# Step sizes behind the first keys, 95 small products ahead of the first Gram, and two value scalings moved to ScalarE

## The chip, the cores and the metric

The kernel runs on one core of a Trainium2 chip. The metric is the device time of one launch in microseconds. Three runs of the kernel before took 745.34, 745.85 and 746.86, median 745.85.

## The reference

Three layers follow each other, all in float32. The first is a delta-rule recurrence over 768 tokens for 4 batches of 8 heads with head size 48; the changed part lies in it:

```python
k_n = k / (np.linalg.norm(k, axis=-1, keepdims=True) + 1e-06)
state = np.zeros((B, H, D, D))
for t in range(S):
    kt, vt, bt = k_n[:, :, t], v[:, :, t], beta[:, :, t, None]
    y[:, :, t] = np.einsum('bhd,bhde->bhe', q[:, :, t], state)
    v_old = np.einsum('bhde,bhd->bhe', state, kt)
    state = state + bt[:, :, :, None] * np.einsum('bhd,bhe->bhde', kt, vt - v_old)
```

A gated layer (384 to 1024, tanh-gelu, a norm, a 768x768 mix over the tokens, 512 to 384, residual) and a second layer with token shift, squared relu and a sigmoid gate follow.

## The kernel before

The recurrence is worked in 12 steps of 64 tokens, two steps to a group. The keys are not normalised; the values are multiplied by the norms of their keys instead. For each group of two steps PE multiplies the keys with each other (`gram`, L320 to L346: two row halves and two block rows per head pair, written as 64x32 products), ScalarE copies the result out of PSUM (L342), and DVE inverts the 32x32 triangles in one long series of small operations (`solver`, L358 to L447). The solver makes the norms first (`neT`, L372), then reads the step sizes `beta_sb` (L380), and ends with a transposed inverse (L440) that PE needs for the group's steps. A product with float32 operands is executed as two products in the trace.

The order of the work on PE, ScalarE, DVE and GpSimd is the order in which the program emits it; each engine takes its own list from the front and waits where an operand is missing. The sync engine's DMA issues are a list of the same kind. At the start the program emits, in this order: the two beta loads (L283), the keys of steps 0 and 1 (L267), memsets of DVE and GpSimd (L299 to L318), two weight blocks (L160), the q of step 0 (L279), values and keys by token of step 0 (L273, L274), and the first Gram in eight jobs. Of these, four jobs for the diagonal blocks come first and feed the solver; the four others feed the coupling of the blocks.

Beside that, weight blocks are split into a rounded part and a rest by "jobs" (`narrow`, L154): a load, a step of ScalarE (L164), four of DVE (L169 to L175), an add on GpSimd (L177), a rounding on ScalarE (L120) and a subtraction on GpSimd (L123). Two jobs are in work at a time, and their steps are strewn between the solver's.

While the first solver is emitted, a list `rest` is emitted beside it, one entry per turn of the loop at L806: the other four jobs of the first Gram, the first products of step 0, and the second group's Gram. The values of steps 0 and 1 are multiplied by their norms in `scale_v` (L464), one GpSimd operation of 128x768 each: step 0 inside the solver (L437), step 1 as the first task after it (L816). The zeros for warm-up products of PE (`keep_warm`, L721) are written by DVE inside the first solver as well (L435).

Of the kernel before, what the change touches and what calls it, by code (L numbers as in the profile page):

```python
# [7 lines left out]
F32 = mybir.dt.float32  # L8
# [3 lines left out]
AF = mybir.ActivationFunctionType  # L12
# [8 lines left out]
P = 128  # L21
C = 64
NG = 6
NU = 32
NPR = 16
# [6 lines left out]
SLOT0 = 3.3  # L32
LOW0 = 1
WARM = 4
SV = 60
B0 = 1.0
PRE = 0.8
GRAM0 = 7
# [35 lines left out]
def vw(t, off, dims):  # L74

    a = t[:]
    return bass.AP(a.tensor, a.offset + off, [list(a.ap[0])] + [list(d) for d in dims])
# [9 lines left out]
def fused_kernel(  # L87
# [17 lines left out]
    nc = tc.nc  # L105
    V, A, G, T = nc.vector, nc.scalar, nc.gpsimd, nc.tensor
# [124 lines left out]
    def slot(tag, shape, dtype=F32):  # L231
        return wq.tile(shape, dtype, name="s" + tag, tag=tag)
# [16 lines left out]
    with ExitStack() as at:  # L249
        ap1 = at.enter_context(tc.tile_pool(name="ap1", bufs=1, side="right"))  # L250
# [8 lines left out]
        kT, kt, vt = {}, {}, {}  # L259
# [3 lines left out]
        def load_k(s):  # L263
            if s >= 12:
                return
            kT[s] = kTb[s % NKT]
            nc.sync.dma_start(out=kT[s], in_=kt_d[s])  # L267

        def load_tok(s):
            t = ap2.tile([P, 2, NPR, D], F32, name="vk")  # L270
            vt[s], kt[s] = t[:, 0], t[:, 1]
            for h in range(2):
                nc.sync.dma_start(out=t[64 * h:64 * h + 64, 0], in_=vk[64 - 64 * h:128 - 64 * h, s, 0])  # L273
            nc.sync.dma_start(out=t[:, 1], in_=vk[:, s, 1])  # L274
# [3 lines left out]
                r = 64 * (1 - h)  # L278
                nc.sync.dma_start(out=SQ[o][s % 2][h][r:r + D, :, D:], in_=q_d[s, o, h])  # L279

        beta_sb = ap1.tile([P, NG, 32], F32, name="beta_sb")
        for h in range(2):
            nc.sync.dma_start(out=beta_sb[64 * h:64 * h + 64], in_=beta[64 - 64 * h:128 - 64 * h])  # L283

        banks = [ps2]

        def bank():
            return banks[0].tile([P, 8, C], F32, name="ms", bufs=3 if banks[0] is ps2 else None)

        Sps = [ps1.tile([P, 8, D], F32, name=f"sps{o}") for o in range(2)]  # L290
        warm = ap1.tile([P, P], mybir.dt.bfloat16, name="warm")
        load_k(0)
        load_k(1)
        NT, GD, Dm = (slot(x, [P, 32, 32]) for x in G0[:3])
        tmp = slot(G0[3], [P, 1024])
        GLb = [slot(G0[4], [P, NU, 32]), slot(W0[2], [P, NU, 32]),
# [52 lines left out]
        GDs, GLs, DTs, neTs, joined = {}, {}, {}, {}, set()  # L349
# [8 lines left out]
        def solver(g):  # L358

            V.transpose(out=NT, in_=GDs[g])  # L360
            G.memset(Yt, 0.0)
            yield 1.14
            ss = ap1.tile([P, 32], F32, name="ss")
            V.tensor_scalar(ss, vw(NT, 0, [(33, 32)]), -1.0, 1e-36, op0=ALU.mult, op1=ALU.max)
            yield 0.2
            ne = yield from rsqrt(ap1, ss, 32, "rn")
            V.tensor_tensor(ne, ne, ss, op=ALU.mult)
            yield 0.2
            V.tensor_scalar(ne, ne, EPS, None, op0=ALU.add)
            yield 0.2  # L370
            neT = ap2.tile([P, 32], F32, name="neT")
            V.transpose(out=neT, in_=ne)  # L372
            neTs[g] = neT
            rn = ap1.tile([P, 32], F32, name="rn")
            V.reciprocal(rn, ne)
            yield 0.4
            V.tensor_tensor(rn, rn, rn, op=ALU.mult)
            yield 0.2
            c = ap1.tile([P, 32], F32, name="c")
            V.tensor_tensor(c, rn, beta_sb[:, g], op=ALU.mult)  # L380
            yield 0.2

            V.tensor_copy(vw(Yt, 0, [(64, 4), (9, 8)]), c.rearrange("p (m i) -> p m i", m=4))
            yield 0.1
            for m in range(4):
                blk = NT[:, 8 * m:8 * m + 8, 8 * m:8 * m + 8]
                V.tensor_tensor(blk, blk, vw(c, 8 * m, [(1, 8), (0, 8)]), op=ALU.mult)
                yield 0.15  # L390

            def total(o_ap, tv, t):
                V.tensor_reduce(out=o_ap, in_=tv, axis=AX.X, op=ALU.add)  # L393
                return t

            for i in range(1, 8):
                tv, t = product(32 * i, [(264, 4), (0, i), (1, i)], NT,
                                0, [(64, 4), (8, i), (1, i)], Yt)
                yield t
                yield total(vw(Yt, i, [(64, 4), (8, i)]), tv, t)  # L400
            V.tensor_copy(vw(Dm, 0, [(264, 4), (32, 8), (1, 8)]), vw(Yt, 0, [(64, 4), (1, 8), (8, 8)]))
            yield 0.4
            V.tensor_copy(vw(NT, 16, [(264, 2), (32, 8), (1, 8)]), vw(Yt, 0, [(64, 2), (8, 8), (1, 8)]))
            yield 0.3
            for dst in (0, 1):
                for p in range(2):
                    o = 16 * p
                    if dst == 0:
                        tv, t = product(32 * (o + 8) + o, [(32, 8), (0, 8), (1, 8)], NT,
                                        128 * p, [(0, 8), (8, 8), (1, 8)], Yt)  # L410
                        ov = vw(NT, 8 + 528 * p, [(1, 8), (32, 8)])
                    else:
                        tv, t = product(33 * (o + 8), [(32, 8), (0, 8), (1, 8)], Dm,
                                        8 + 528 * p, [(0, 8), (32, 8), (1, 8)], NT)
                        ov = vw(Dm, 32 * (o + 8) + o, [(32, 8), (1, 8)])
                    yield t
                    yield total(ov, tv, t)
                    if dst and p == 0:
                        V.tensor_copy(vw(NT, 24, [(1, 8), (32, 8)]), ov)
                        yield 0.2  # L420
            for last in (0, 1):
                if last == 0:
                    ops = [(vw(Yt, 16 * j, [(1, 16), (16, 4)]),
                            (32 * 16 + j, [(32, 16), (0, 4), (1, 16 - j)], NT,
                             16 + 33 * j, [(0, 16), (32, 4), (1, 16 - j)], NT))
                           for j in (12, 8, 4, 0)]
                else:
                    ops = [(vw(Dm, 32 * (16 + i), [(32, 4), (1, 16)]),
                            (32 * (16 + i) + 16, [(32, 4), (0, 16), (1, i + 4)], Dm,
                             0, [(0, 4), (16, 16), (1, i + 4)], Yt)) for i in (0, 4, 8, 12)]  # L430
                for i, (ov, args) in enumerate(ops):
                    tv, t = product(*args)
                    yield t
                    if g == 0 and last and i == 1:
                        V.memset(warm, 0.0)  # L435
                    if g == 0 and last and i == 2:
                        scale_v(0)  # L437
                    yield total(ov, tv, t)
            DT = DTb[g % 2]
            V.transpose(out=DT.rearrange("p u i -> p i u"), in_=Dm)  # L440
            DTs[g] = DT
            yield 1.14
            if g:
                p = point[0] + LAGC
                p += -p % 6 if p % 6 > 2 else 0
                for k in range(2):
                    later.append((p + 6 * k, lambda k=k: couple(g, k)))  # L447
# [16 lines left out]
        def scale_v(s):  # L464
            G.tensor_tensor(vt[s], vt[s], vw(neTs[s // 2], NPR * (s % 2), [(1, NPR), (0, D)]),
                            op=ALU.mult)

        RQs, ysts = {}, {}

# [127 lines left out]
        def after(n, f):  # L597
            later.append((point[0] + n, f))
# [187 lines left out]
        for o in range(2):  # L786
            load_q(0, o)
        load_tok(0)
        diag = gram(0, ((0, 32), (32, 64)))
        for job in diag[:4]:  # L790
            for _, f in job:
                f()
            early(1, NPRE)
        streams.append([point[0], solver(0), "solve"])
        for s in range(2, NKT):
            load_k(s)

        def whole(job):
            for _, f in job:
                f()  # L800
# [3 lines left out]
        rest = [lambda j=j: whole(j) for j in diag[4:]]  # L804
        k = 0
        while any(e[2] == "solve" for e in streams):  # L806
            early(1, PRE)
            k += 1
            if k == 2:
                load_tok(1)  # L810
                for o in range(2):
                    load_q(1, o)
                nc.sync.dma_start(out=g_sb, in_=g_ln)
                nc.sync.dma_start(out=mu_sb, in_=mu)
            if 0 in neTs and 1 not in GDs:
                after(SV, lambda: scale_v(1))  # L816
                body = st_rq(0, 0)
                rest.append(lambda: next(body))
                rest += [lambda j=j: whole(j) for j in gram(1)]
            if rest:  # L820
                rest.pop(0)()
        for f in rest:
# [420 lines left out]
```

## Time and profile before

| | |
|---|---|
| runs (us) | 745.34, 745.85, 746.86 |
| span of the profiled execution (us) | 745.5; no other time of it is given |
| PE busy | 690.3 us, 93%, 10832 products |
| DVE, ScalarE, GpSimd busy | 514.1, 367.9, 201.6 us |
| granted clock over the span | 0.982 |

PE is the busiest engine, but busy time is a mean over stages with different limits. The first of the 40 slices of the span show PE at 2 to 9 tenths and DVE at 6 to 9, the last twenty PE at 9. The span counts from the first to the last instruction of the profiled execution.

### The profile page before, as it was taken

The page shows a single profiled execution, that of the slowest core. Times are in us where ns is not written, and L with a number is a line of the kernel's source. Part 1 is how long each engine was busy: PE and PEld are TensorE (multiplying, and loading weights), DVE is VectorE, ACT ScalarE, POOL GpSimd, SP SyncE. Part 2 cuts the span into 40 slices and gives each one's busy share as a digit, 9 for nine tenths or more (in the row PEclk, how much of TensorE's full clock was granted, in tenths as well). Part 3 has the DMA queues.
Part 4 walks back from the last instruction along what each step waited for, and adds up shares of the span by engine and source line. Part 5 has one row for each costly group of instructions (what it writes and reads, how often), then busy time and mean ns, then how long its engine had stood idle before and what let it go on. Part 6 is the DMA issues. An engine that isn't in the chain of part 4 may idle for free.

```text
span 745.5 us, 24942 instructions
## 1 busy us (share of the span) xinstructions
PE 690.3 (93%) x10832; PEld 641.5 (86%) x10832; DVE 514.1 (69%) x1070; ACT 367.9 (49%) x752; POOL 201.6 (27%) x253
## 2 busy tenths in 40 slices
PE   2668789999998999899999999999999999999998
PEld 2537568878886987779999999999999999999997
DVE  6989999898998695642476857599556565563341
ACT  2226656766675676774331413149445354452240
POOL 3033534454444265463131515330000000000000
PEclk9988989999999899999999999999999999999999
DMA  8503443575565565848763645268000000000000
GB/s 237 133 30 85 130 109 102 165 211 144 144 193 146 151 185 160 231 139 234 236 229 103 189 134 168 84 204 222 33 11 21 33 11 23 22 11 32 16 17 33
DMA packets 81550, 88.76 MB, mean 119 GB/s; under 512 B 24704, under 2 KB 64320, under 8 KB 81440
## 3 DMA queue, kind: packets, MB, share of 16 engines
q1 hardware_dynamic: 76384, 77.72, 35.2%
q0 software_dynamic: 5056, 9.44, 4.7%
q8 instruction: 85, 1.39, 0.8%
q14 instruction: 25, 0.20, 0.1%
HBM read 56.60 MB, written 25.82 MB: 111 GB/s over the span
## 4 chain that ended last, share of the span: by engine, by line
PE 74%; DVE 17%; issue 3%; ACT 2%; DMA 1%; POOL 1%; SPq 1%; POOLq 0%; DVEq 0%; ACTq 0%
PE ms L151 39%; PE ms L960 13%; PE ms L687 5%; DVE sg L355 5%; PE ms L635 4%; DVE sg L393 3%; PE ms L563 2%; DVE Yt L393 2%; PE rk L521 1%; PE ms L456 1%; PE rk L534 1%; PE sps L549 1%; PE rk L498 1%; PE ms L333 1%; PE ms L726 1%
## 5 line engine op out<-in xcount | busy, mean ns | idle before, releaser
L151 PE MATMUL ms<-wvh,sl 128*128 128x384 f32 x192 | 64.6, 336 | 0.0
L151 PE MATMUL ms<-wvl,sh 128*128 128x384 f32 x192 | 64.5, 336 | 0.0
L151 PE MATMUL ms<-wvh,sh 128*128 128x384 f32 x192 | 64.5, 336 | 0.0
L151 PE MATMUL ms<-xm_hi,sw0h 128*128 128x384 f32 x192 | 64.2, 335 | 0.0
L151 PE MATMUL ms<-xm_hi,sw0l 128*128 128x384 f32 x192 | 64.2, 334 | 0.0
L151 PE MATMUL ms<-xm_lo,sw0h 128*128 128x384 f32 x192 | 64.2, 334 | 0.0
L1059 ACT ACTIVATE gh<-w 128x384 fp32r<-128x384 f32 x32 | 16.8, 526 | 93.4 <-DVE w L1058 93.4
L177 POOL TENSOR_TENSOR na<-na,raw 128x256 int32<-128x256 int32 (+2 forms) x43 | 36.5, 849 | 96.0 <-ACT gh L1059 40.7
L123 DVE TENSOR_TENSOR sl<-sg,sh 128x384 fp32r<-128x384 f32 x64 | 35.7, 558 | 30.2 <-ACT sh L120 30.2
L120 ACT ACTIVATE sh<-sg 128x384 fp32r<-128x384 f32 x64 | 33.5, 524 | 36.4 <-DVE sg L1163 36.4
L960 PE MATMUL ms<-sw0h,g 128*128 128x384 f32 x192 | 50.2, 335 | 0.0
L960 PE MATMUL ms<-ws1h,g 128*128 128x384 f32 x192 | 49.9, 334 | 0.0
L355 DVE TENSOR_TENSOR sg<-sg,Yt 128x512 f32<-128x512 f32 (+10 forms) x78 | 46.8, 599 | 1.8
L1179 DVE TENSOR_TENSOR sg<-sg,ms 128x384 f32<-128x384 f32 x24 | 13.3, 555 | 44.9 <-PE ms L151 44.9
L1163 DVE TENSOR_TENSOR sg<-sg 128x384 f32<-128x384 f32 x64 | 35.4, 553 | 10.9 <-ACT sg L1162 10.9
L1162 ACT ACTIVATE sg<-ms 128x384 f32<-128x384 f32 x64 | 30.7, 480 | 22.9 <-PE ms L151 22.9
L514 POOL TENSOR_SCALAR_AFFINE_SELECT SQ<-SQ 64x512 f32<-64x512 f32 x36 | 27.0, 749 | 50.9 <-ACT SQ L513 49.8
L120 ACT ACTIVATE xm_hi<-sg 128x384 fp32r<-128x384 f32 x48 | 23.1, 517 | 34.6 <-PE ms L151 30.5
L687 PE MATMUL ms<-xl,wiu_hi 128*128 128x256 f32 x144 | 39.7, 297 | 0.0
L687 PE MATMUL ms<-xh,wiu_lo 128*128 128x256 f32 x144 | 38.7, 292 | 0.1
L333 PEld LDWEIGHTS ms<-kT 64*32 64x32 f32 x640 | 20.0, 131 | 21.7 <-issue 13.9
L335 PE MATMUL ms<-kT 64*32 64x64 f32 (+1 forms) x640 | 23.3, 235 | 16.5 <-issue 16.5
(246 smaller groups left out, 2241.1 us busy)
## 6 DMA issues: line engine op xcount, KB each, us to landing
u_d<-ug SPq DMA_DIRECT2D x24, 256.0 KB, 4.6
u<-u_d SPq DMA_DIRECT2D x16, 384.0 KB, 4.3
vn_d<-v SPq DMA_DIRECT2D x22, 256.0 KB, 2.8
vk<-in_vk_dram SPq DMA_DIRECT2D x24, 192.0 KB, 3.6
vk<-in_vk_dram SPq DMA_DIRECT2D x12, 384.0 KB, 4.5
out_dram<-sg SPq DMA_DIRECT2D x24, 192.0 KB, 1.9
kT<-in_kt_d_dram SPq DMA_DIRECT2D x8, 512.0 KB
SQ<-in_q_d_dram SPq DMA_DIRECT2D x36, 96.0 KB, 4.0
```

Source lines behind the costliest of these rows:

```text
L120: A.activation(hi, src, AF.Copy)
L123: eng_lo.tensor_tensor(lo, src, hi.bitcast(F32), op=ALU.subtract)
L151: T.matmul(pt, lhsT=a, rhs=b, start=(i == 0), stop=(i == n - 1))
L177: G.tensor_tensor(a.bitcast(I32), a.bitcast(I32), w_lo.bitcast(I32), op=ALU.add)
L333: T.matmul(gps[r:r + 32, p, c0:c1], lhsT=t[r:r + 64, u, 0:32], rhs=t[r:r + 64, u, c0:c1], start=True, stop=True)
L355: V.tensor_tensor(tv, vw(a_t, a_off, a_dims), vw(b_t, b_off, b_dims), op=ALU.mult)
L393: V.tensor_reduce(out=o_ap, in_=tv, axis=AX.X, op=ALU.add)
L635: T.matmul(vstat[g, b], lhsT=a[:, c], rhs=w[:, c], start=first, stop=last)
L687: T.matmul(vstat["u"][:, 2 * P * d:2 * P * d + 2 * P], lhsT=w[:, c, ds_], rhs=a[:, c].rearrange("p b t -> p (b t)"), start=first, stop=last)
L960: T.matmul(pt[:, :DM], lhsT=v[:, ds_], rhs=w, start=(c == 0 and i == 0), stop=(c == 5 and i == 2))
L1162: A.activation(r, pt[:, :DM], AF.Relu)
L1163: V.tensor_tensor(r, r, r, op=ALU.mult)
```

## The change

The two beta loads are issued after the first loads of values, keys and q. The zeros are written first thing, and 95 products of 32 rows by 32 by 8 columns of these zeros are emitted ahead of all other products of PE. The two GpSimd operations that scale the values of steps 0 and 1 become 32 ScalarE operations, one per step and head pair (128x48), emitted in eight parts of four at the end of the list `rest`; later steps are scaled by GpSimd as before.

```diff
-SV = 60
+NLEAD = 95
...
-        beta_sb = ap1.tile([P, NG, 32], F32, name="beta_sb")
-        for h in range(2):
-            nc.sync.dma_start(out=beta_sb[64 * h:64 * h + 64], in_=beta[64 - 64 * h:128 - 64 * h])
...
+        V.memset(warm, 0.0)
         load_k(0)
         load_k(1)
+        beta_sb = ap1.tile([P, NG, 32], F32, name="beta_sb")
+
+        def load_beta():
+            for h in range(2):
+                nc.sync.dma_start(out=beta_sb[64 * h:64 * h + 64], in_=beta[64 - 64 * h:128 - 64 * h])
+
+        o = bank()
+        for i in range(NLEAD):
+            b0 = 32 * (i % 4)
+            T.matmul(o[b0:b0 + 32, i // 4 % 8, 0:8], lhsT=warm[b0:b0 + 32, 0:32],
+                     rhs=warm[b0:b0 + 32, 0:8], start=True, stop=True)
...
-                    if g == 0 and last and i == 1:
-                        V.memset(warm, 0.0)
-                    if g == 0 and last and i == 2:
-                        scale_v(0)
...
+        def scale_act(s, u0, n):
+            for u in range(u0, u0 + n):
+                A.activation(vt[s][:, u, :], vt[s][:, u, :], AF.Identity,
+                             scale=neTs[s // 2][:, NPR * (s % 2) + u:NPR * (s % 2) + u + 1])
...
         load_tok(0)
+        load_beta()
         diag = gram(0, ((0, 32), (32, 64)))
...
             if 0 in neTs and 1 not in GDs:
-                after(SV, lambda: scale_v(1))
                 body = st_rq(0, 0)
                 rest.append(lambda: next(body))
                 rest += [lambda j=j: whole(j) for j in gram(1)]
+                rest += [lambda s=s, u=u: scale_act(s, u, 4) for s in range(2) for u in range(0, NPR, 4)]
```

## Rows read from the trace of the kernel before

**Rows 1.** The page: instruction queue (packets, MB, share), and the chain's shares.

```profile
q8 instruction: 85, 1.39, 0.8%
...
PE 74%; DVE 17%; issue 3%; ACT 2%; DMA 1%; POOL 1%; SPq 1%; POOLq 0%; DVEq 0%; ACTq 0%
```

**Rows 2.** Chain of waits, 0 to 100 us: start, us, what.

```profile
48.93 0.78 POOL na L177
...
50.98 0.29 DVE na L169
...
95.47 1.92 PE ms L456 x64
```

**Rows 3.** Timeline of the sync engine's issues: start, us, line, tile, count.

```profile
0.80 1.22 SPq L283 DMA_DIRECT2D beta_sb<-in_beta_dram  x2
...
10.82 0.59 SPq L274 DMA_DIRECT2D vk<-in_vk_dram  x1
```

**Rows 4.** Timeline of DVE; in brackets the idle time before, and its releaser.

```profile
9.40 0.29 DVE L169 TENSOR_SCALAR na<-raw 128x256 uint32<-128x256 uint32 x1 [0.79 <-DMA raw<-in_w_in_dram]
...
14.68 1.25 DVE L360 STREAM_TRANSPOSE sg<-sg 128x1024 f32<-128x1024 f32 x1 [3.50 <-ACT sg L342]
...
19.57 1.33 DVE L377 TENSOR_TENSOR rn<-rn 128x32 f32<-128x32 f32 x1
20.94 0.19 DVE L380 TENSOR_TENSOR c<-rn,beta_sb 128x32 f32<-128x32 f32 x1
...
54.20 0.43 DVE L364 TENSOR_SCALAR ss<-sg 128x32 f32<-128x32 f32 x1
```

**Rows 5.** Timeline of ScalarE.

```profile
9.75 0.60 ACT L342 ACTIVATE sg<-ms 128x256 f32<-128x256 f32 x1
11.80 0.42 ACT L120 ACTIVATE wiv_hi<-na 128x256 fp32r<-128x256 f32 x1 [1.45 <-POOL na L177]
...
14.06 0.80 ACT L342 ACTIVATE sg<-ms 128x256 f32<-128x256 f32 x2
...
37.24 0.43 ACT L342 ACTIVATE sw0h<-ms 128x256 f32<-128x256 f32 x1
46.41 0.42 ACT L120 ACTIVATE wiv_hi<-na 128x256 fp32r<-128x256 f32 x1 [8.74 <-POOL na L177]
```

**Rows 6.** DMA issues, 0 to 62 us: size of one, median us to landing.

```profile
raw<-in_w_in_dram SPq DMA_DIRECT2D x9, 256.0 KB, 4.6
...
vk<-in_vk_dram SPq DMA_DIRECT2D x2, 384.0 KB, 7.5
```

**Rows 7.** Windows of PE: stretch, length, busy (products), granted clock, DMA share, GB/s.

```profile
0.00:9.50 9.50, 3.20 (x223) 1.00 0.68 208
9.50:18.40 8.90, 1.93 (x128) 1.00 0.94 263
18.40:26.00 7.60, 1.93 (x128) 1.00 1.05 243
```

**Rows 8.** Timeline of PE: the first products after two stops.

```profile
12.06 0.21 PE L335 MATMUL ms<-kT 64*32 64x32 f32 x1 [2.70 <-issue]
...
18.53 0.21 PE L335 MATMUL ms<-kT 64*32 64x32 f32 x1 [4.55 <-issue]
```

**Rows 9.** Timeline of GpSimd.

```profile
19.39 1.47 POOL L465 TENSOR_TENSOR vk<-vk,neT 128x768 f32<-128x768 f32 x1 [4.18 <-DVE neT L372]
...
46.90 0.73 POOL L123 TENSOR_TENSOR wiv_lo<-na,wiv_hi 128x256 fp32r<-128x256 f32 x1 [0.53 <-ACT wiv_hi L120]
```

**Rows 10.** ScalarE grouped by form (busy us, mean ns), and one timeline row.

```profile
L1141 ACT ACTIVATE sg<-xT,m_sb 128x384 f32<-128x384 f32 x48 | 26.3, 606 | 0.7 <-DVE xm_lo L123 0.7
L671 ACT ACTIVATE v<-v,nm,rs 128x512 f32<-128x512 f32 x24 | 19.2, 804 | 2.1 <-POOL nm L667 2.1
L120 ACT ACTIVATE xh<-xT 128x768 fp32r<-128x768 f32 x12 | 10.1, 840 | 0.0
...
549.11 1.62 ACT L1141 ACTIVATE sg<-xT,m_sb 128x384 f32<-128x384 f32 x3
```

## What the change will do, predicted before it ran

> **What bounds the kernel now.** I read the page's chain shares first, then the chain of waits from 0 to 100 us, then each engine's timeline up to 62 us, then PE's windows. PE holds 74% of the chain and DVE 17% [rows 1]. DVE's share is one block at the front: it runs the first two triangular solves almost without a gap until PE takes the chain over at 95.47 [rows 2]. From there the program is the same list of products whatever happened before. So I price each part of the change by how much earlier or later DVE, and so PE at 95.47, arrives, and then ask what else moves.
>
> Inside that block I use three places. The first solve starts at 14.68, after a wait of 3.50 for ScalarE's eviction of the fourth Gram job [rows 4]. That eviction, at 14.06, stands in ScalarE's queue behind two roundings of the weight jobs, which wait for GpSimd [rows 5]. Near the end of the solve ScalarE, GpSimd and DVE pass the same weight jobs on: DVE's load step at 50.98 waits until GpSimd has finished job 4, whose add began at 48.93 [rows 2].
>
> **Beta behind the keys.** The two beta issues take the sync engine from 0.80 for 1.22 us [rows 3]. They go behind the first values and keys, so the first keys and the first two weight blocks are issued 1.22 earlier. The q loads of the second state pair wait for a DVE memset and gain nothing. DVE's second weight step waited 0.79 for its block at 9.40 [rows 4]; that wait goes, the step before it being bound by DVE's memsets. Everything down to 14.06 hangs on it, so the solve can start 0.8 earlier. The beta load itself now goes out after the load issued at 10.82 for 0.59 [rows 3], so at about 11.4 to 12.6; behind it the next weight blocks, keys and q loads go out up to 1.22 later, none needed within 3 us of landing. Beta is read at 20.94 [rows 4], about 19 after the change. Loads of this stretch land 4.6 (weight blocks) to 7.5 us (keys) after issue [rows 6], that is at 16.0 to 20.1: cost 0 to 1.1, taken as 0, since the weight blocks issued next to it are the nearer row.
>
> **95 products.** Each is a weight load and a product, 190 instructions. PE is not in the chain before 95.47, so neither their own time nor a faster clock for the Gram is worth anything directly. What they take is room in the instruction stream. PE executed 223 products up to 9.50, then exactly 128 before 18.40 and 128 before 26.00 [rows 7]; between them it stood 2.70 and 4.55 us with no releaser but "issue" [rows 8]. 128 products are 256 instructions, and the page has a queue of 85 instruction packets of 16 KB (1.39 MB) [rows 1]. I read it so: PE runs out of code, and a piece of 256 instructions arrives every 6.5 us here. Four Gram jobs are 256 products; the stop before 12.06 falls in the fourth. With 95 products ahead, the stop falls after 223-95 = 128: in front of the third job.
>
> Whether that costs depends on when the next piece arrives. The first stretch began at 12.06 - 2.70 - 3.20 = 6.16 with the landing of the keys [rows 7, 8]; its first 96 products (223 less a piece) were through at 6.16 + 96 x 3.20/223 = 7.5, and the next piece arrived 4.5 us later. The new products are issued as soon as a memset of zeros is through, and fill 95 of those 96 places before the keys land; so the request goes out between 3 us and that landing, now at 6.16 - 1.22 = 4.9. With 4.5 to 6.5 us for a piece it arrives between 7.5 and 11.4; I take 9.5. Then the third job's 64 products (half of 1.93 [rows 7]) and its eviction (0.60 [rows 5]) with 0.2 between end at 11.3, and the rounding that started at 11.80 [rows 5] can start there: 0.5 earlier instead of 0.8. I take **-0.55**. The bounds are -0.8 (piece before 9.2) and +2.0 (piece at 12.06, rounding at 13.8).
>
> By the Trainium skill ("Runtime: NRT & Kernel Launch", section "Instruction fetch mechanics") code comes in 16 KiB blocks of 256 instructions, fetched while the current block runs, and crossing a block is mostly hidden. The size agrees with this trace; "hidden" does not, with 2.70 and 4.55 us of standing. By the page the start would be -0.8 and the sum 0.25 better.
>
> All later piece boundaries move by 190 of 256 instructions. "Issue" holds 3% of the chain [rows 1], and part of it after 95 us is this; which dense stretch meets a boundary is re-dealt. I count 0 and keep +-2 for the range.
>
> **Value scaling off GpSimd.** GpSimd's product of values and norms ran from 19.39 for 1.47 [rows 9]. DVE's square of 128x32, issued at 19.57, took 1.33, while the product of the same size after it took 0.19 [rows 4]: it ended with GpSimd's. Both sit on the chain, so **-1.14**. The second one lay ahead of the second solve, where one 128x32 step took 0.43 at 54.20 instead of 0.19 [rows 4]: **-0.24**.
>
> ScalarE gets 32 instructions of 128x48 in place of these. They stand behind the second pair's Gram evictions, whose last ran at 37.24 for 0.43 [rows 5], and ahead of the rounding at 46.41. Price of one: 768 columns take 840 ns [rows 10] and 256 take 0.42 us [rows 5], so 0.82 ns a column; three scalings with a per-partition factor, 384 columns each, take 1.62 together and one 0.606 [rows 10], so they follow each other every 0.507. Less 336 columns, 0.231 each, 7.4 us together. A bias counted as a second operand gives (804 ns of the 512-column form [rows 10], less 0.098 overlap and 464 columns) 0.325, or 10.4; one with no factor at all about 0.14, or 4.5. They begin at about 38.4: 37.7 as before, plus 0.7, because the last Gram job now lies in one more piece of code (bounds 36 and 40). They end at 45.8, from 42.9 to 48.8. The deadline: GpSimd's add of job 4, at 48.93, will want to run 1.9 earlier, at 47.0, and ahead of it stand the rounding of job 3 (0.49 from 46.41 to GpSimd's start) and GpSimd's subtraction (0.73) [rows 5, 9]: 45.8, less 0.2 for gaps, is where the rounding has to start. Taken: **+0.2** late, bounds 0 and +3.2. The values of step 0 are then ready by 42, ahead of DVE's result at about 46.7, so PE doesn't wait; the zero fill of the warm-up tile only moves from inside the solve to the memsets in front, both on DVE's path, net 0.
>
> **Sum.** -0.55 - 1.14 - 0.24 + 0.2 = -1.7 on the profiled span of 745.5, so 743.8; the median of the runs stands 0.35 above that span: 744.1.
>
> **Rivals.**
> 1. Code arrives early and ScalarE is done in time: -0.8 - 1.14 - 0.24, and the re-dealt boundaries give 2 back: -4.2, 741.7. For it: the request goes out 3 to 4 us earlier; against: a sum of lucky ends. Chance 0.14.
> 2. The third Gram job waits for code: the piece comes only at 11.4, the solve starts 1.35 later than now (11.4 + 0.97 + 0.2 + 0.6 against 11.80), and the gains at GpSimd pay for it: 1.35 - 1.38 + 0.2, about 0.2 above now, 746.0. For it: every piece between 12 and 26 took 6.5 us or more. Against: at 3 to 5 us fewer loads are in flight. With smaller mixes of the same kind that end within 1 us of now, chance 0.27.
> 3. **Slower:** ScalarE's queue. The scalings hold the rounding of job 3, and through GpSimd the whole of DVE's second solve. Each microsecond of end after 45.6 is a microsecond lost; at 0.285 each (end 47.5) the gain is gone, and 0.332 each makes it slower by 1.5. At 0.36, between my 0.231 and the 0.507 of the full 384 columns, they end at 49.9, 4.3 late: -1.93 + 4.3 = +2.4, 748.2. For it: 32 small instructions, each with a pointer operand, in a queue that was idle 8.74 us there and no more [rows 5]. Against: the price per column. Chance 0.12.
> 4. That the products do nothing of use (no code sooner, no clock) leaves the second rival's numbers; it has no time of its own.
>
> **How the numbers follow.** The forecast, -1 to -3, has 0.47; its own range is 742.8 to 744.9. 0.2% is 1.5 us, and is about what can be told from no change. Faster by more than that (below 744.35): the first rival's 0.14 and 0.38 of the forecast's 0.47, together 0.52. Slower: the third rival's 0.12. Same: the second's 0.27 and the forecast's other 0.09, 0.36. The range takes in the first rival and the second, and stops short of the third: 741.2 to 746.8.
>
> **What would show it.** DVE's 128x32 square at about 19 us back to 0.19. The first transposition of the solve at 13.9 to 14.3. PE's first stop in front of the third Gram job, and its end well before 11. 32 short ScalarE rows of 0.32 each, every 0.23, over before 46, and the rounding behind them not waiting for them. PE's chain at about 93.7 instead of 95.47. Wrong if the solve starts after 14.68, if the rounding of job 3 starts straight behind the last scaling after 46, or if PE after 95 stands for code 2 us more or less than now.

## The result, and the profile after

The changed kernel takes 750.2 us (median of 13 runs, 746.41 to 756.96) against 745.85 for the kernel before on the same chip (13 runs, 743.03 to 749.46). The ratio is 1.0062, with a 95% interval of 1.004 to 1.0084. So it is slower, by about 4.6 us, where 744.1 was forecast. The execution that was profiled took 746.41, the shortest of the 13. Its trace therefore shows less of the loss than the median does; the experiments show the rest.

The page of the changed kernel, against [rows 1]: the span, the instruction queue, the chain's shares.

```profile
span 744.6 us, 25161 instructions
...
q8 instruction: 85, 1.39, 0.8%
...
PE 80%; DVE 11%; issue 3%; DMA 3%; ACT 1%; POOL 1%; SPq 1%; POOLq 0%; ACTq 0%; DVEq 0%
```

DVE's share of the chain has fallen from 17% to 11%, and PE's has risen from 74% to 80%. Most of that is another path and no gain: DVE's busy time fell only from 514.1 to 511.8 us, while the chain now runs through PE from 49 to 81 us. Issue is still 3%. That share alone would not tell anyone where the time went.

The timeline of DVE after, for [rows 4]: start, us, engine, line, operation; in brackets the idle time before and what ended it.

```profile
8.93 0.29 DVE L169 TENSOR_SCALAR na<-raw 128x256 uint32<-128x256 uint32 x1 [0.36 <-DMA raw<-in_w_in_dram]
...
14.20 1.25 DVE L368 STREAM_TRANSPOSE sg<-sg 128x1024 f32<-128x1024 f32 x1 [3.50 <-ACT sg L350]
...
19.09 0.19 DVE L385 TENSOR_TENSOR rn<-rn 128x32 f32<-128x32 f32 x1
...
52.76 0.19 DVE L372 TENSOR_SCALAR ss<-sg 128x32 f32<-128x32 f32 x1
```

The wait for the weight block is 0.36 instead of 0.79, and the solve starts 0.48 sooner. The square of 128x32 is back at 0.19 from 1.33, and the later 128x32 step at 0.19 from 0.43.

The timeline of ScalarE after, for [rows 5]: the 32 scalings in one row, and the rounding behind them.

```profile
35.60 7.29 ACT L474 ACTIVATE vk<-vk,neT 128x48 f32<-128x48 f32 x32
44.77 0.42 ACT L120 ACTIVATE wiv_hi<-na 128x256 fp32r<-128x256 f32 x1 [1.88 <-POOL na L177]
```

7.29 over 32 is 0.228 each. They end at 42.9; the rounding then waits 1.88 for GpSimd, not for them.

The timeline of PE after, its first rows and two stops, for [rows 8].

```profile
1.04 0.91 PE L300 MATMUL ms<-warm 32*32 32x8 bf16 x95 [1.04 <-DVE warm L288]
4.36 0.26 PE L341 MATMUL ms<-kT 64*32 64x32 f32 x1 [2.41 <-DMA kT<-in_kt_d_dram]
...
7.65 0.26 PE L341 MATMUL ms<-kT 64*32 64x32 f32 x1 [1.37 <-issue]
...
16.48 0.26 PE L341 MATMUL ms<-kT 64*32 64x32 f32 x1 [2.62 <-issue]
```

The 95 products are through by 1.95. PE's first stop has moved forward: it now comes after 128 Gram products and ends at 7.65. The code for the third job came in time.

The chain of waits after, one stop on the way and the place where PE takes over, for [rows 2].

```profile
61.89 2.58 issue
...
94.01 0.30 DVE na L169
...
94.33 1.92 PE ms L460 x64
```

PE takes over at 94.33 instead of 95.47, 1.14 sooner. So the front kept about two thirds of the 1.7 that was forecast. What follows loses that as well. Each solve ends in a transposition that releases PE; here are the fourth and the fifth in DVE's timelines, first of the kernel before.

```profile
189.93 2.00 DVE L440 STREAM_TRANSPOSE DT<-sg 128x1024 f32<-128x1024 f32 x1
...
238.37 1.94 DVE L440 STREAM_TRANSPOSE sw0l<-sg 128x1024 f32<-128x1024 f32 x1
```

The same two in the kernel after.

```profile
186.26 1.93 DVE L444 STREAM_TRANSPOSE DT<-sg 128x1024 f32<-128x1024 f32 x1
...
238.48 1.93 DVE L444 STREAM_TRANSPOSE sw0l<-sg 128x1024 f32<-128x1024 f32 x1
```

After is 3.67 us ahead at 186 and 0.11 behind at 238. Start to start this stretch takes 48.44 before and 52.22 after. In between, PE stands with no releaser but "issue". PE's timeline after, the four stops of that stretch and one more at 301:

```profile
200.12 0.32 PE L460 MATMUL ms<-DT,sg 32*32 32x32 f32 x9 [0.24 <-issue]
...
205.05 0.44 PE L530 MATMUL rk<-r,DT 32*32 32x48 f32 x18 [0.68 <-issue]
...
210.93 0.24 PE L343 MATMUL ms<-kT 64*32 64x64 f32 x1 [1.24 <-issue]
...
216.31 0.39 PE L696 MATMUL ms<-xh,wiu_lo 128*128 128x256 f32 x1 [1.34 <-issue]
...
301.59 0.50 PE L644 MATMUL ms<-wiv_lo,xh 128*128 128x512 f32 x1 [0.94 <-issue]
```

The four make 0.24 + 0.68 + 1.24 + 1.34 = 3.50, and with a shorter one 3.7. The kernel before has 0.7 of such stops in the same stretch. So they account for 3.0 of the 3.78 us that the stretch has grown by; the rest is that PE waits 2.1 instead of 1.3 for DVE's transposition at its start. PE's windows over the stretch (length, busy, products, granted clock, DMA share, GB/s), the kernel before:

```profile
189.93:238.37 48.44, 44.75 (x1388) 1.00 0.58 163
```

The kernel after:

```profile
186.26:238.48 52.22, 44.71 (x1380) 1.00 0.55 152
```

PE is busy for the same time at the same clock. It does not run slower, it stands longer. The stops lie about 5 to 6 us apart, and none of these products has anything to do with the change. That made code pieces that arrive late the suspect.

### The profile page after: what moved, and what is told of

Its sections match the earlier page's. It is cut to its first block, busy times and chain, and to the rows that moved or that the text cites. A ratio compares the mean times of both kernels' runs of the same rounds, so it can differ in the third digit from the quotient of the medians.

```text
span 744.6 us, 25161 instructions
## 1 busy us (share of the span) xinstructions
PE 691.8 (93%) x10927; PEld 642.9 (86%) x10927; DVE 511.8 (69%) x1070; ACT 374.8 (50%) x784; POOL 199.4 (27%) x251
## 4 chain that ended last, share of the span: by engine, by line
PE 80%; DVE 11%; issue 3%; DMA 3%; ACT 1%; POOL 1%; SPq 1%; POOLq 0%; ACTq 0%; DVEq 0%
PE ms L151 39%; PE ms L970 13%; PE ms L696 6%; PE ms L644 5%; DVE sg L363 3%; PE ms L572 2%; DVE sg L401 2%; PE rk L530 2%; PE ms L460 2%; PE rk L543 2%; PE sps L558 2%; PE ms L341 2%; PE rk L507 2%; PE ms L735 1%; DMA raw<-in_w_in_dram 1%
## 5 line engine op out<-in xcount | busy, mean ns | idle before, releaser
L970 PE MATMUL ms<-ws1h,g 128*128 128x384 f32 x192 | 49.9, 334 | 0.0
L523 POOL TENSOR_SCALAR_AFFINE_SELECT SQ<-SQ 64x512 f32<-64x512 f32 x36 | 27.2, 755 | 50.1 <-ACT SQ L522 49.0
L696 PE MATMUL ms<-xh,wiu_lo 128*128 128x256 f32 x144 | 38.7, 291 | 1.3 <-issue 1.3
L696 PE MATMUL ms<-xl,wiu_hi 128*128 128x256 f32 x144 | 39.6, 296 | 0.0
L696 PE MATMUL ms<-xh,wiu_hi 128*128 128x256 f32 x144 | 38.4, 289 | 0.0
L401 DVE TENSOR_REDUCE sg<-sg 128x64 f32<-128x512 f32 (+3 forms) x48 | 35.9, 747 | 0.9
```

The costliest lines, as they stand in the source:

```text
L523: G.affine_select(out=pt, in_=pt, pattern=[[0, 8], [1, C]], compare_op=ALU.is_gt, fill=0.0, base=0, channel_multiplier=-1)
L696: T.matmul(vstat["u"][:, 2 * P * d:2 * P * d + 2 * P], lhsT=w[:, c, ds_], rhs=a[:, c].rearrange("p b t -> p (b t)"), start=first, stop=last)
L970: T.matmul(pt[:, :DM], lhsT=v[:, ds_], rhs=w, start=(c == 0 and i == 0), stop=(c == 5 and i == 2))
```

## The experiments

Theory A: the 190 instructions of the 95 products shift every later piece of 256 instructions by 190 against the work, and at the new positions PE stands longer. Only the number of instructions ahead, modulo 256 (128 products), should count. Theory B: ScalarE's scalings or the moved beta loads are what is slow. Theory C: the products change PE's clock at the front. A fourth theory has no letter in the expectations: the products cost by their own number or their place (the front is held up, or the load on the instruction queue).

All ratios are to the kernel before in alternating runs on the same chip. The first four kernels ran together on one chip (the kernel before: 748.15), the next four on another (747.9), the last four on a third (747.46). The expected times of the first four were written with the 745.85 above in mind, so there the ratios compare better.

**No products, beta and scalings kept.**

```diff
-NLEAD = 95
+NLEAD = 0
```

> The changed kernel without the 95 products; beta behind the keys and the scalings on ScalarE stay. Theory A (code pieces: the 190 instructions move every later boundary of PE's instruction pieces, and the dense Gram and value stretches between 160 and 240 us now meet them): boundaries fall as before the change, so only the gains are left, 743.5 to 745 us. Theory B (the ScalarE scalings or the later beta cost the time): still 749 to 751. Theory C (the products change PE's clock at the front): 743.5 to 745, as A.

745.7 us, ratio 0.998 (0.9954 to 1.0005). On the same chip the unchanged kernel after took 750.5 (below). So the products cost 750.5 - 745.7 = 4.8 us, and beta and scalings are worth -2.45 by the medians, with an interval that just reaches no change. By the ratios the products cost 4.2. Theory B falls.

**128 products, one whole piece.**

```diff
-NLEAD = 95
+NLEAD = 128
```

> The changed kernel with 128 products instead of 95: 256 instructions, one whole piece, so that all later boundaries fall on the same instructions as before the change. Theory A: 743.5 to 745.5 us. Theory B: 749 to 751. Theory C: as slow as with 95 or slower, 750 or more. This run tells A from C.

746.05 us, ratio 0.9971 (0.995 to 0.9993). A third more products than 95, and the cost is gone. The more the dearer falls with this run, and so does C, by which 128 had to be as slow as 95.

**The products alone,** in the kernel before.

```diff
+NLEAD = 95
...
+        V.memset(warm, 0.0)
...
+        o = bank()
+        for i in range(NLEAD):
+            b0 = 32 * (i % 4)
+            T.matmul(o[b0:b0 + 32, i // 4 % 8, 0:8], lhsT=warm[b0:b0 + 32, 0:32],
+                     rhs=warm[b0:b0 + 32, 0:8], start=True, stop=True)
...
-                    if g == 0 and last and i == 1:
-                        V.memset(warm, 0.0)
```

> The kernel before with the zeros and the 95 products in front as the only edit; beta first, values scaled by GpSimd. Theory A: slower than before by at least the 4.3 us of the change, 750 to 752 us, since the gains of the other parts are missing. Theory B: 745 to 747. Theory C: 750 to 752.

755.99 us (six runs), ratio 1.0102 (1.0076 to 1.0129), above the 750 to 752 expected by A. By itself this part costs 7.8 us by the medians, beside the others 4.8. The loss is the products'. Each of the two figures is uncertain by 2 us or more, so whether the parts add up stays open.

**The kernel after again,** unchanged.

> The changed kernel once more, for a second trace of it and for its time on the same chip as the other three. 749 to 751 us by all theories. The first trace was of an execution of 746.4, faster than nearly all the others. Theory A: where this trace is slower than the first, PE stands for code (idle released by nothing but issue) between 100 and 330 us. Theory C: a stretch at granted 0.5 lies over products on the chain there.

750.5 us, ratio 1.0036 (1.0012 to 1.0059). Slower again, by somewhat less than at first. Its profiled execution took 749.77, nearer to its median than the first one did, and PE's timeline has four of the five stops again; the one at L530 is missing.

```profile
204.83 0.32 PE L460 MATMUL ms<-DT,sg 32*32 32x32 f32 x9 [1.00 <-issue]
...
214.27 0.24 PE L343 MATMUL ms<-kT 64*32 64x64 f32 x1 [0.41 <-issue]
218.82 0.39 PE L696 MATMUL ms<-xh,wiu_lo 128*128 128x256 f32 x1 [0.52 <-issue]
...
304.96 0.50 PE L644 MATMUL ms<-wiv_lo,xh 128*128 128x512 f32 x1 [2.40 <-issue]
```

The places come back; how long PE stands at each differs from execution to execution (0.94 and 2.40 at the last), and at some it does not stand at all. The granted clock over the stretch is 0.97 here and 1.00 in the first trace after.

**33 more products later,** behind the warm-up products of step JS, where they run at 43.3 us (95 + 33 = 128).

```diff
+NLATE = 33
...
+        o = bank()
+        for i in range(NLATE):
+            b0 = 32 * (i % 4)
+            T.matmul(o[b0:b0 + 32, i // 4 % 8, 0:8], lhsT=warm[b0:b0 + 32, 0:32],
+                     rhs=warm[b0:b0 + 32, 0:8], start=True, stop=True)
```

> The changed kernel with 33 more of the same small products behind the 18 warm-up products ahead of step 0's solve products, where PE waits for DVE anyway. Front as in the changed kernel; from there on 128 products, 256 instructions, are ahead of everything, so the piece boundaries of the dense part fall as before the change. If the boundaries of the dense part cost the time: ratio to before 0.995 to 0.999, as with 128 in front (0.9971). If the 95 products hurt by what they do at the front: 1.003 to 1.007, as the change.

746.73 us, ratio 0.9995 (0.9971 to 1.002). The loss does not show although the front is that of the kernel after, 95 products included. More work, added later, made up for it. The ratio came just above the expected range.

**All 95 later,** the loop taken from the front to that place.

> The changed kernel with its 95 products moved behind the 18 warm-up products; nothing in front of the first Gram. Front as before the change, boundaries of the dense part as in the changed kernel. If the boundaries of the dense part cost the time: ratio to before 1.003 to 1.008. If the products hurt at the front: 0.995 to 0.999, as without them (0.998).

752.04 us, ratio 1.0046 (1.002 to 1.0072), 5.3 us above the kernel with 95 and 33 on the same chip. With no product at the front the loss is there in full. With the run before, this shows that it is the shift of what follows, not what the products do in front of the Gram, and not a clock that they change there.

**The scalings alone,** in the kernel before.

```diff
-                    if g == 0 and last and i == 2:
-                        scale_v(0)
...
+        def scale_act(s, u0, n):
+            for u in range(u0, u0 + n):
+                A.activation(vt[s][:, u, :], vt[s][:, u, :], AF.Identity,
+                             scale=neTs[s // 2][:, NPR * (s % 2) + u:NPR * (s % 2) + u + 1])
...
-                after(SV, lambda: scale_v(1))
...
+                rest += [lambda s=s, u=u: scale_act(s, u, 4) for s in range(2) for u in range(0, NPR, 4)]
```

> The kernel before with the ScalarE scalings in place of GpSimd's as the only edit. By the prediction's terms -1.14 - 0.24 us, DVE's 128x32 square back at 0.19, ratio 0.998; if ScalarE's queue costs at the end of the first solve, 1.000 or more. In the changed kernel's trace the scalings ran from 35.6 to 42.9, so no cost is expected.

745.22 us, ratio 0.9967 (0.9942 to 0.9992): faster than the kernel before. DVE's timeline shows the term that was forecast for it.

```profile
19.92 0.19 DVE L377 TENSOR_TENSOR rn<-rn 128x32 f32<-128x32 f32 x1
20.15 0.19 DVE L380 TENSOR_TENSOR c<-rn,beta_sb 128x32 f32<-128x32 f32 x1
```

And ScalarE's timeline shows the queue that the third rival feared.

```profile
38.15 7.29 ACT L468 ACTIVATE vk<-vk,neT 128x48 f32<-128x48 f32 x32
45.60 0.42 ACT L120 ACTIVATE wiv_hi<-na 128x256 fp32r<-128x256 f32 x1 [0.16 <-POOL na L177]
```

Here the scalings end at 45.44 and the rounding starts 0.16 later, released by GpSimd. There was next to no room left, and nothing was lost.

**The beta loads alone,** moved behind the first values and keys.

```diff
-        for h in range(2):
-            nc.sync.dma_start(out=beta_sb[64 * h:64 * h + 64], in_=beta[64 - 64 * h:128 - 64 * h])
...
         load_tok(0)
+        for h in range(2):
+            nc.sync.dma_start(out=beta_sb[64 * h:64 * h + 64], in_=beta[64 - 64 * h:128 - 64 * h])
```

> The kernel before with the beta loads behind the first values and keys as the only edit. By the prediction's term the first solve starts 0.5 to 0.8 us earlier, ratio 0.999; a later landing of beta or of the loads behind it would make it 1.000 to 1.002.

746.4 us, ratio 0.9978 (0.9952 to 1.0003): about 1.5 us better by the medians, which the interval doesn't tell from nothing.

**The sweep.** The same kernel after with 32, 64, 112 and 223 products in place of 95. 223 is 95 + 128, so it leaves later pieces at the positions of 95, one piece further on.

```diff
-NLEAD = 95
+NLEAD = 32
```

> The changed kernel with 32 products in front: later boundaries move by 64 of 256 instructions. Boundaries theory: any value between the two seen (0.997 to 1.006), since a quarter of a piece has not been tried; theory that more products cost more: between 0.998 (none) and 1.004 (95), about 1.000. Taken: 0.997 to 1.000, a candidate to beat both kernels.

> The changed kernel with 64 products in front: boundaries moved by half a piece. Boundaries theory: a value of its own between 0.997 and 1.006; theory that more products cost more: about 1.002.

> The changed kernel with 112 products in front: boundaries moved by 224 of 256, between the 95 (1.0036 and 1.0062) and the 128 (0.9971). Boundaries theory: between these two, 0.999 to 1.003. Theory that more products cost more: 1.005 or above.

> The changed kernel with 223 products in front, 95 + 128: one whole piece more than the change, so the same later boundaries on the same instructions. Boundaries theory: as slow as with 95, 1.003 to 1.007, by the period of 128. Against it: with two pieces of the front used up before the keys land, anything near 0.998 would say that the position of the boundaries is not the cause.

32: 747.34 us, 0.9997 (0.9968 to 1.0026). 64: 747.76, 1.0002 (0.997 to 1.0034). 112: 750.74, 1.0043 (1.0011 to 1.0075), a little above what was expected. 223: 755.91, 1.0101 (1.0066 to 1.0135), slow as the period asks, but by more than expected. The period itself shows in the PE timeline of 223 products: it stops before the very instructions at which the kernel after does.

```profile
209.14 0.32 PE L460 MATMUL ms<-DT,sg 32*32 32x32 f32 x9 [0.77 <-issue]
213.79 0.44 PE L530 MATMUL rk<-r,DT 32*32 32x48 f32 x18 [0.41 <-issue]
219.95 0.24 PE L343 MATMUL ms<-kT 64*32 64x64 f32 x1 [1.51 <-issue]
225.05 0.38 PE L696 MATMUL ms<-xh,wiu_lo 128*128 128x256 f32 x1 [1.07 <-issue]
...
313.11 0.50 PE L644 MATMUL ms<-wiv_lo,xh 128*128 128x512 f32 x1 [2.02 <-issue]
```

L460 x9, L530 x18, L343, L696 and L644 are the same products, 128 tiny ones further from the start. The kernel before, those without products and with 128 have a position of their own in common: PE stops before the one product of line L498 of the kernel before (L507 after). The kernel before, in PE's timeline:

```profile
215.63 0.25 PE L498 MATMUL rk<-SQ,kT 64*64 64x48 f32 x1 [0.26 <-issue]
```

The same instruction with no products:

```profile
209.74 0.20 PE L507 MATMUL rk<-SQ,kT 64*64 64x48 f32 x1 [0.48 <-issue]
```

And with 128 products:

```profile
215.47 0.25 PE L507 MATMUL rk<-SQ,kT 64*64 64x48 f32 x1 [0.81 <-issue]
```

The kernels with 95 and 33 later, with the scalings alone and with beta alone stop before it as well (0.53, 0.25 and 1.06).

The plainest evidence is a count. PE's windows from 0 to two stops of the kernel before (the products in brackets):

```profile
0.00:211.50 211.50, 169.31 (x5450) 0.95 0.51 140
0.00:215.60 215.60, 173.06 (x5578) 0.95 0.52 142
```

And from 0 to two stops of the kernel after, other products of the program:

```profile
0.00:205.00 205.00, 166.69 (x5451) 0.93 0.51 140
0.00:210.90 210.90, 171.34 (x5578) 0.93 0.51 142
```

Counted from PE's first product, the added ones included, both kernels stop at the same numbers. It is so in all fourteen traces: the 114 stops of over 0.2 us with releaser "issue" that come after 95 us stand on one grid, whose steps are 127 or 128 products. So these stops belong to the pieces of code, and added products move the program along the grid.

How long PE waits between 95 and 345 us (PE's waits in that window; whom for: us in total, times, longest). With no products:

```profile
PE sps L558 <- issue: 1.2, 3, 0.6
...
PE rk L507 <- issue: 0.5, 1, 0.5
PE ms L343 <- issue: 0.4, 1, 0.4
...
PE ms L572 <- issue: 0.2, 1, 0.2
```

With 223 products:

```profile
PE ms L343 <- issue: 2.9, 3, 1.5
...
PE ms L644 <- issue: 2.0, 1, 2.0
PE ms L572 <- issue: 1.9, 2, 1.2
PE rk L530 <- issue: 1.5, 2, 1.1
PE rk L507 <- issue: 1.3, 2, 1.1
PE ms L696 <- issue: 1.1, 1, 1.1
PE qk L510 <- issue: 1.0, 2, 0.6
PE ms L460 <- issue: 0.8, 1, 0.8
```

2.3 us in all against 12.5. These two traces are far ends: the first is the shortest of its 12 executions (741.3), the second the third longest of 10 (758.05). Over all traces, PE's stops of this kind after 95 us come to 2.3 to 7.9 in the six kernels whose added products make a whole piece or none (4.7 on average), and to 5.8 to 12.5 in the five shifted by 95 (8.6).

One stretch sums it up: from the fourth of those transpositions to the fifth, start to start, in the profiled execution of every kernel. The phase is the count of added products modulo 128, at the front or anywhere ahead of that stretch; the columns are the stretch in us, PE's granted clock in it, and the ratio of that kernel's runs.

```
phase 0:   none, beta and scalings     48.2     1.00     0.998
           kernel before               48.4     1.00
           128 at the front            48.7     1.00     0.9971
           scalings alone              49.6     0.93     0.9967
           95 and 33 later             49.9     1.00     0.9995
           beta alone                  50.1     0.97     0.9978
phase 95:  kernel after                52.2     1.00     1.0062
           95 alone                    52.4     1.00     1.0102
           kernel after again          52.5     0.97     1.0036
           223                         53.9     0.97     1.0101
           95 later                    54.5     0.94     1.0046
others:    64                          50.1     1.00     1.0002
           32                          52.7     0.94     0.9997
           112                         55.2     0.91     1.0043
```

Six kernels of phase 0 take 48.2 to 50.1, five of phase 95 take 52.2 to 54.5, with no overlap, wherever the products stand and whatever else is changed. The means are 49.1 and 53.1: 4.0 us from this one stretch, out of 4.8 by the two medians on the first chip. The clock is not the cause: where it is 1.00, phase 0 takes 48.2 to 49.9 and phase 95 takes 52.2 and 52.4. Within phase 95, and with 32 and 112 products, the longest stretches go with the lowest clocks, so part of them is the clock. The stretch was picked in the first trace after, because it had grown there; the other traces are the test. From the sixth transposition to the end both phases take 459.4 on average. Each row is one execution; the 52.7 of 32 products comes from an execution of 752.06, where that kernel's median is 747.34.

## Why the prediction was wrong

**The step that failed** is "All later piece boundaries move by 190 of 256 instructions. [...] which dense stretch meets a boundary is re-dealt. I count 0 and keep +-2 for the range." The mechanism was named and mis-sized: the products cost 4.8 us by the medians on one chip, and 4.0 show in one stretch, twice the bound of 2. That outweighed the whole rest of the change. By the prediction's own sign ("if PE after 95 stands for code 2 us more or less than now"), PE's stops after 95 us came to 4.6 before, to 5.8 in the first trace after, from its shortest execution, and to 8.1 in the second. The premise beneath, "From there the program is the same list of products whatever happened before", holds for the list and not for where its code is cut. The bound is not worked out from any row; beside it stands only "issue" at 3% of the chain. A share of the page says what the positions of one program cost, not what another set costs: that share is 3% after too, while such stops in one stretch grew from 0.7 to 3.7 us. The Trainium skill ("Runtime: NRT & Kernel Launch", section "Instruction fetch mechanics") has code come in blocks of 256 instructions and calls their crossing mostly hidden. The period of 128 products of two instructions agrees with the block; stops of 0.24 to 2.40 us deep in the kernel don't agree with hidden.

The other steps, by the trace after:

- Beta and the products at the front: the solve starts 0.48 sooner, where 0.55 was forecast, but that is luck. With beta moved alone it starts at 13.49, 1.19 sooner than before. With the 95 in front it starts at 14.20, 14.21 and 14.29 in three traces, against 13.57 and 13.58 with none in front and beta and scalings kept. So beta was worth about 1.2, not 0.8, and the products cost about 0.6, not 0.25. Nor did they cost by way of the code, counted at 9.5: it came at 7.65. DVE's second weight block set the time; DVE waits 0.36 for it after, and no such wait shows with beta alone. Why the block is late behind the products was not tested.
- GpSimd: -1.14 stands exactly; the square takes 1.33 wherever GpSimd still scales (95 alone, beta alone) and 0.19 where ScalarE does. The -0.24 is there too, but is not shown to be due to the scalings: with beta alone, where GpSimd still scales, that step took 0.19 as well.
- ScalarE: 7.29 for 32, where 7.4 was worked out. They begin at 35.60, not 38.4 and outside the bounds of 36 and 40, and at 35.51 in the kernel without products; the 0.7 counted for one more piece of code did not come, and the +0.2 is nothing. Even at 38.15, in the kernel with scalings alone, the rounding behind them starts only 0.16 after them, released by GpSimd. By the Trainium skill ("ScalarE: Activation LUTs", section "What ACT_TABLE_LOAD costs") 48 columns with one pointer operand, overlapped, come to an estimate of 226 ns; the trace has 228.
- Sum of the front: at the end of the first solve -1.64 (its last transposition starts at 45.03 instead of 46.67), where the terms due by then make -1.69; beta's luck is in it. At 94.33 it is -1.14. The 0.5 lost in between goes with the products too: from the first transposition to the second, the four kernels without any take 46.0 to 46.7 and the ten with some 47.1 to 48.3, whatever their number or place. What causes it was not tested. In the chain after, PE and not DVE holds most of the way from 49 to 81, and it has a stop of 2.58 of its own there (61.89 in the chain above).
- Rivals: the third had the side right and the mechanism wrong, since ScalarE's queue costs nothing. The second, that the third job waits for code, is refuted by 7.65. The first counted re-dealt positions as a possible gain of 2. They were a loss.

**Open.** Why the pieces at the positions of 95 products come late more often was not tested. The loads that share the DMA engines are an obvious candidate, but no run varied them. Nor is it known whether the 95 really cost more alone (7.8 us) than in company (4.8), or why 223 cost more than 95: in its trace the first two solves end 2.5 and 3.5 us later than after (47.50 and 95.72 against 45.03 and 92.27), so part of it is the front. Executions of one kernel spread by 4 to 12 us here; the intervals come from many of them.

## What to carry to other kernels

On a kernel whose TensorE streams code for most of its span, count the instructions that a change adds ahead of the dense part, modulo the size of a code piece, and price that shift as a term with bounds as wide as all "issue" of the dense part (here 4.6 us after 95 us in the kernel before). Before keeping such a change, time it with a whole piece of filler too: 128 products instead of 95 gave 0.9971 (0.995 to 0.9993) where 95 gave 1.0036 (1.0012 to 1.0059) on the same chip. The scalings without any products, 0.9967 (0.9942 to 0.9992), are the simplest version that beats both kernels.

## What the runs showed of the hardware

- The count of PE instructions ahead, modulo 256, moved the time by 0.4 to 1.0%: 190 more cost it, 256 more cost nothing that shows (0.9971 against 0.998 without any).
- In fourteen traces PE's stops without a releaser, after 95 us, come at the same counts of products from the start, 127 or 128 apart (5451 and 5578, for example), whatever the products are.
- At such a place PE stands for a different time in each execution: 0.94 and 2.40 us at the same product in two executions of one kernel.
- 32 short ScalarE operations with a per-partition factor (128x48) follow each other every 0.228 us, and took 7.29 in both traces shown here.
- One profiled execution can hide most of an effect: 746.41 in the first trace after, with a median of 750.2, where the kernel before has 745.85.
